# One head's rows of wo through six DMA engines, three heads of the last group as 1 KB rows

## The chip, the cores and the metric

The kernel runs on one core of a Trainium2 chip. The metric is the device time of one execution in microseconds (us). Executions of one kernel do not agree exactly, so a comparison here is of several executions of two kernels in alternation on one chip. A ratio is the mean time of one kernel's fast runs over that of the other's fast runs of the same rounds, so it is not quite the ratio of the medians quoted beside it.

## The reference

Decode attention with grouped heads over a window of 512 cached positions, then the output projection:

```python
B, Sq, D = 32, 1, 512;  Hq, Hkv, Sk, Dh = 32, 8, 2048, 128;  W = 512
q = (x @ wq).reshape(B, Sq, Hq, Dh)
scores = q . k[:, :, Sk-W:] * Dh**-0.5;  p = softmax(scores);  o = p @ v[:, :, Sk-W:]
out = o.reshape(B, Sq, Hq*Dh) @ wo          # wo: 4096 x 512, bf16, 4 MB
```

The bytes are 33.6 MB each of K and V, 4.2 MB each of wq and wo: 75.5 MB, nearly all read once.

## The kernel before: the parts that matter

The last thing loaded is wo, eight groups of 512 rows (one group = four heads). A partition takes four neighbouring rows, one piece of 4 KB. Because of that a partition m holds rows 4m to 4m+3, and the attention output must be brought into the same order: a *selection* by matmuls with a band of ones gives `o_sel[m, i, group, batch]`.

```python
            sp.wait_ge(pe_PV, 2 * Z_HOME.rindex("w") + 2)
            for hg in range(NHG):                       # NHG = 8 groups
                for i0, i1 in ((0, 4),) if hg < NHG - 1 else ((0, WO_CUT), (WO_CUT, 4)):
                    sp.dma_start(wo_sb[:, hg, i0:i1]..., wo[hg*512:(hg+1)*512, :].rearrange("(m i) n -> m (i n)", i=4)...)
                      .then_inc(sem_last if i0 else sem_wo[hg], 16)
# ... TensorE, after the last V chunk (V15) has been used:
            select(SELCUT, B, ...)                      # 4 x 4 matmuls, 128x128 weights
            pe.wait_ge(dve_sel, 2); pe.wait_ge(act_sel, 2)
            for hg in range(NHG):
                pe.wait_ge(sem_wo[hg], 16)
                for i in range(4):
                    if hg == NHG - 1 and i == WO_CUT:   # WO_CUT = 3
                        pe.wait_ge(sem_last, 16)
                    for c in range(2):                  # two halves of 256 columns
                        pe.matmul(X_ps[32*c:32*(c+1), 2, 0:256], lhsT=o_sel[:, i, hg, :], rhs=wo_sb[:, hg, i, c*256:(c+1)*256], ...)
```

A selection of the first 24 batches is done earlier, the last 8 batches only after V15.

Of the kernel before, what the change touches and what calls it, by code (L numbers as in the profile page):

```python
# [5 lines left out]
BF16 = mybir.dt.bfloat16  # L6
F32 = mybir.dt.float32
ACTF = mybir.ActivationFunctionType
ALU = mybir.AluOpType
# [3 lines left out]
def bass_standalone__sliding_block_cached__sampling_kernel(  # L13
# [8 lines left out]
    B, Sq, D = x.shape  # L22
    _, HKV, SK, DH = k_cache.shape
    HD = wq.shape[1]
    HQ = HD // DH
# [19 lines left out]
    RING = 3  # L45
    WO_CUT = 3
    XD = 20
# [24 lines left out]
    with ExitStack() as es:  # L72
# [12 lines left out]
        pick = sb("pick", [P, REP, KS + P], BF16)  # L85
        mask = sb("mask", [P, NBG], F32)
        oT_sb = sb("oT_sb", [P, HQ, B], BF16)
        ident = sb("ident", [32, 32], BF16)
# [7 lines left out]
        K_0 = K_sb[:, 0].rearrange("p r d -> p (r d)")  # L96
        o_sel = K_0[:, 0:HQ * B].rearrange("p (i g b) -> p i g b", i=4, g=NHG)
        band = K_0[:, HQ * B:HQ * B + 4 * 224].rearrange("p (i n) -> p i n", i=4)
        oT_flat = oT_sb[:, :, :].rearrange("p h b -> p (h b)")
# [22 lines left out]
        sem_wq = [sem(f"sem_wq{i}") for i in range(2)]  # L122
        sem_wo = [sem(f"sem_wo{i}") for i in range(NHG)]
        sem_last = sem("sem_last")
        sem_k = [sem(f"sem_k{i}") for i in range(NK)]
# [31 lines left out]
        pool_band = sem("pool_band")  # L157
        pool_qbd = sem("pool_qbd")
        nc.scalar.dma_start(x_sb, x.rearrange("b s d -> b (s d)")).then_inc(sem_x, 16)
        wq_rows = wq.rearrange("(p t) n -> p (t n)", t=DKT)  # L160
# [16 lines left out]
        def z_waits(eng, q):  # L177
# [7 lines left out]
            else:  # L185
                eng.wait_ge(pe_S, NQUAD)

        def cache_rows(cache, m, k=1):
            q, e = divmod(m, 2)
            rows = cache[4 * q:4 * q + 4, :, SK - W:, :].rearrange("b g (s r) d -> (b g) s (r d)", s=KS)  # L190
            return rows[:, :, e * CR * DH:(e + k) * CR * DH]

        @block.sync
        def _(sp):
# [19 lines left out]
            sp.wait_ge(pe_PV, 2 * Z_HOME.rindex("w") + 2)  # L214
            for hg in range(NHG):
                for i0, i1 in ((0, 4),) if hg < NHG - 1 else ((0, WO_CUT), (WO_CUT, 4)):
                    sp.dma_start(  # L217
                        wo_sb[:, hg, i0:i1].rearrange("p i n -> p (i n)"),
                        wo[hg * 512:(hg + 1) * 512, :].rearrange("(m i) n -> m (i n)", i=4)[:, i0 * 512:i1 * 512],
                    ).then_inc(sem_last if i0 else sem_wo[hg], 16)  # L220
            sp.wait_ge(dve_out, 1)
# [7 lines left out]
        def _(pool):  # L229
# [43 lines left out]
            for q in range(NQUAD):  # L273
# [3 lines left out]
            pool.memset(band[:, :, :], 0.0).then_inc(pool_band, 1)  # L277
            pool.wait_ge(pool_band, 1)
            pool.affine_select(
                out=band[:, :, :], in_=band[:, :, :], compare_op=ALU.not_equal, fill=1.0,  # L280
                base=384, pattern=[[-1, 4], [-4, 224]], channel_multiplier=1,
            ).then_inc(pool_band, 1)

        @block.tensor
        def _(pe):
# [82 lines left out]

            def select(b0, b1, dst):
                pe.wait_ge(act_O, min(b1 // 4, NQUAD - 1))  # L370
                if b1 == B:
                    pe.wait_ge(dve_O, 1)
                for i in range(4):
                    for hi in range(4):
                        ins = pe.matmul(
                            dst(i),
                            lhsT=band[:, i, 96 - 32 * hi:224 - 32 * hi],
                            rhs=oT_sb[:, :, b0:b1].rearrange("p (g hi) b -> p hi g b", hi=4)[:, hi],
                            start=(hi == 0), stop=(hi == 3), tile_position=(0, 0), skip_group_check=True,
                        )  # L380
                ins.then_inc(pe_sel, 1)

            for name in PE_ORDER:
                k = int(name[1:])
                {"S": scores, "P": p_turn, "V": pv}[name[0]](k)
                if name == "V12":
                    pe.wait_ge(pool_band, 2)
                    nb = SELCUT
                    select(0, nb, lambda i: X_ps[:, i // 2, (i % 2) * NHG * nb:(i % 2 + 1) * NHG * nb])
            nl = B - SELCUT  # L390
            select(SELCUT, B, lambda i: S_ps[:, i // 2, (i % 2) * NHG * nl:(i % 2 + 1) * NHG * nl])
            pe.wait_ge(dve_sel, 2)
            pe.wait_ge(act_sel, 2)
            for hg in range(NHG):
                pe.wait_ge(sem_wo[hg], 16)
                for i in range(4):
                    if hg == NHG - 1 and i == WO_CUT:
                        pe.wait_ge(sem_last, 16)
                    for c in range(2):
                        ins = pe.matmul(  # L400
                            X_ps[32 * c:32 * (c + 1), 2, 0:256],
                            lhsT=o_sel[:, i, hg, :],
                            rhs=wo_sb[:, hg, i, c * 256:(c + 1) * 256],
                            start=(hg == 0 and i == 0), stop=(hg == NHG - 1 and i == 3),
                            tile_position=(0, 32 * c),
                        )
            ins.then_inc(pe_fin, 1)

        @block.vector
        def _(dve):  # L410
# [62 lines left out]
            def sel_evac(src, i0, ni, b0, b1):  # L473
                return (
                    o_sel[:, i0:i0 + ni, :, b0:b1],
                    src[:, 0:ni * NHG * (b1 - b0)].rearrange("p (i g b) -> p i g b", i=ni, g=NHG),
                )

            dve.wait_ge(pe_sel, 1)
            dve.tensor_copy(*sel_evac(X_ps[:, 0], 0, 2, 0, SELCUT)).then_inc(dve_sel, 1)  # L480
            dve.wait_ge(pe_PV, NCH)
            dve.tensor_copy(  # L482
# [3 lines left out]
            dve.wait_ge(pe_sel, 2)  # L486
            dve.tensor_copy(*sel_evac(S_ps[:, 0], 0, 2, SELCUT, B)).then_inc(dve_sel, 1)
            dve.wait_ge(pe_fin, 1)
            dve.tensor_copy(out_sb[:, 0, :], X_ps[0:32, 2, 0:256]).then_inc(dve_out, 1)

        @block.scalar
        def _(act):
# [52 lines left out]
            for name in ACT_ORDER:  # L545
                arg = [int(a) for a in name[1:].split(".")]
                {"E": soften, "N": norm, "C": pt_evac, "O": o_evac, "Z": spread}[name[0]](*arg)
                if name == "Z7.3":
                    act.wait_ge(pe_sel, 1)
                    act.activation(  # L550
                        o_sel[:, 2:4, :, 0:SELCUT],
                        X_ps[:, 1, 0:2 * NHG * SELCUT].rearrange("p (i g b) -> p i g b", i=2, g=NHG),
                        ACTF.Copy,
                    ).then_inc(act_sel, 1)
            nl = B - SELCUT
            act.wait_ge(pe_sel, 2)
            act.activation(
                o_sel[:, 2:4, :, SELCUT:B],
                S_ps[:, 1, 0:2 * NHG * nl].rearrange("p (i g b) -> p i g b", i=2, g=NHG),
                ACTF.Copy,  # L560
            ).then_inc(act_sel, 1)
            act.wait_ge(pe_fin, 1)
            act.activation(out_sb[:, 1, :], X_ps[32:64, 2, 0:256], ACTF.Copy).then_inc(act_out, 1)
# [28 lines left out]
```

## Time and profile before

| | before |
|---|---|
| median time | 187.2 us (187.12 to 187.27) |
| span of the profiled run | 185.5 us |
| HBM read | 75.53 MB, 407 GB/s over the span |
| last V load landed, its first matmul | 172.57 us, 172.70 us |
| last wo load landed, TensorE's end | 182.72 us, 183.06 us |

Times within a run count from the start of the span. The prediction below shows the lines that carry the reading. Two things that no view prints are taken from the trace directly: how long single DMA packets took (a packet is one record of the trace's DMA part, with its size and duration), and the completions. In the trace every large load has 16 completions, each with its time. I call them *landings* and read each as one DMA engine's: the page counts 16 DMA engines, and the distances between landings hold from load to load (the last of the 16 lies 3.39 to 3.44 us behind the first in each of the first seven groups of wo). I count a load as there at its last landing: V15's last landing before is 172.57 us, its first matmul starts at 172.70.

### The profile page before, as it was taken

What the parts mean: (1) busy time and instruction counts of PE and PEld (TensorE: products, weight loads), DVE (VectorE), ACT (ScalarE), POOL (GpSimd) and SP (SyncE); (2) the same over time, 40 slices, a digit from 0 to 9 for tenths busy, and PEclk for the clock granted to TensorE, in tenths of its full rate; (3) what the DMA queues carried; (4) which work ended last, traced back from release to release, by engine and by line L of the source; (5) the groups of instructions that cost most, each with busy time, mean ns of one, the idle gap of its engine ahead of it and who ended that gap; (6) DMA issues with size and microseconds to landing.
All of it is one profiled execution on the core that took longest, in us unless ns stands there. A gap on an engine that the chain in (4) does not pass through costs nothing.

```text
span 185.5 us, 3711 instructions
## 1 busy us (share of the span) xinstructions
PE 109.5 (59%) x1540; PEld 90.3 (49%) x1540; DVE 132.1 (71%) x239; ACT 81.2 (44%) x141; POOL 31.8 (17%) x82
## 2 busy tenths in 40 slices
PE   0220303454469704994430899155999989998773
PEld 0100001141369403974130878014998888997761
DVE  0018699979799799979999269999999975510020
ACT  3000100129900686027941005965939999961000
POOL 7100029515300250042330015000003000000000
PEclk9999999999559965799965599755599999999999
DMA  6999999989999999999999999989999999999980
GB/s 201 428 445 424 431 421 484 445 367 424 424 421 445 413 435 421 428 435 410 458 438 392 445 410 442 463 382 442 415 431 431 410 438 417 438 410 416 400 338 30
DMA packets 5872, 75.80 MB, mean 409 GB/s; under 512 B 672, under 2 KB 864, under 8 KB 1888
## 3 DMA queue, kind: packets, MB, share of 16 engines
q1 hardware_dynamic: 5808, 75.53, 96.5%
q8 instruction: 12, 0.20, 0.4%
q10 hardware_dynamic: 48, 0.03, 0.1%
q14 instruction: 4, 0.03, 0.0%
HBM read 75.53 MB, written 0.03 MB: 407 GB/s over the span
## 4 chain that ended last, share of the span: by engine, by line
DMA 41%; PE 22%; DVE 20%; ACT 7%; issue 6%; SPq 3%
PE O_ps L361 16%; DMA V_sb<-in_v_cache_dram 11%; DMA w_sb<-in_wo_dram 11%; DVE KT_sb L439 10%; DMA K_sb<-in_k_cache_dram 10%; DMA w_sb<-in_wq_dram 9%; DVE w_sb L461 5%; PE S_ps L322 4%; ACT w_sb L530 4%; DVE QA_sb L429 2%; SPq L217 2%; ACT KT_sb L530 1%; PE PT_ps L341 1%; DVE maxv L446 1%; PE X_ps L302 1%
## 5 line engine op out<-in xcount | busy, mean ns | idle before, releaser
L439 DVE STREAM_TRANSPOSE KT_sb<-K_sb 128x2048 uint32<-128x2048 uint32 x32 | 72.5, 2290 | 12.9 <-DMA K_sb<-in_k_cache_dram 12.9
L361 PE MATMUL O_ps<-w_sb,V_sb 128*128 128x128 bf16 x640 | 45.4, 240 | 10.0 <-DVE w_sb L461 5.1
L361 PEld LDWEIGHTS O_ps<-w_sb,V_sb 128*128 128x128 bf16 x640 | 44.2, 108 | 12.0 <-issue 6.1
L271 POOL COPY QBD<-QA_sb 32x64 bf16<-32x64 bf16 x64 | 25.5, 539 | 83.0 <-PE S_ps L322 60.5
L530 ACT ACTIVATE w_sb<-PTc,mask 128x512 bf16<-128x512 bf16 x60 | 38.7, 725 | 0.0
L461 DVE TENSOR_SCALAR w_sb<-PTc,mask 128x512 bf16<-128x512 bf16 x100 | 31.1, 379 | 2.3 <-ACT PTc L521 1.1
L322 PE MATMUL S_ps<-KT_sb,QBD 128*32 128x512 bf16 x256 | 20.2, 465 | 18.2 <-POOL QBD L271 11.0
L341 PE MATMUL PT_ps<-P_bf,pick 128*128 128x128 bf16 x128 | 12.6, 277 | 24.6 <-ACT P_bf L511 20.0
L341 PEld LDWEIGHTS PT_ps<-P_bf,pick 128*128 128x128 bf16 x128 | 10.9, 128 | 28.2 <-ACT P_bf L511 22.8
L502 ACT ACTIVATE X_ps<-S_ps,negmax 128x512 f32<-128x512 f32 x8 | 5.2, 649 | 39.5 <-DVE negmax L448 39.5
L322 PEld LDWEIGHTS S_ps<-KT_sb,QBD 128*32 128x32 bf16 x256 | 7.5, 108 | 27.7 <-POOL QBD L271 11.9
L361 PE MATMUL O_ps<-K_sb,V_sb 128*128 128x128 bf16 x256 | 15.1, 217 | 2.3 <-DMA V_sb<-in_v_cache_dram 2.3
L530 ACT ACTIVATE K_sb<-PTc,mask 128x512 bf16<-128x512 bf16 x24 | 15.3, 717 | 1.6 <-DVE KT_sb L439 1.6
L361 PEld LDWEIGHTS O_ps<-K_sb,V_sb 128*128 128x128 bf16 x256 | 14.5, 96 | 3.1 <-issue 3.1
L540 ACT ACTIVATE oT_sb<-O_ps 128x128 bf16<-128x128 f32 x7 | 5.2, 742 | 16.9 <-PE O_ps L361 16.9
L461 DVE TENSOR_SCALAR K_sb<-PTc,mask 128x512 bf16<-128x512 bf16 x40 | 10.7, 346 | 2.4 <-ACT PTc L521 2.4
L302 PE MATMUL X_ps<-w_sb,oT_sb 128*32 128x512 bf16 x32 | 3.8, 627 | 10.6 <-DMA w_sb<-in_wq_dram 10.6
L482 DVE CAST oT_sb<-O_ps 128x128 bf16<-128x128 f32 x1 | 0.7, 711 | 12.9 <-PE O_ps L361 12.9
L496 ACT ACTIVATE KT_sb<-X_ps 128x512 bf16<-128x512 f32 x1 | 0.6, 597 | 17.3 <-PE X_ps L302 17.3
L511 ACT ACTIVATE P_bf<-X_ps,recip 128x512 bf16<-128x512 f32 x8 | 5.5, 682 | 6.0 <-DVE recip L454 6.0
L530 ACT ACTIVATE KT_sb<-PTc,mask 128x512 bf16<-128x512 bf16 x12 | 8.0, 726 | 0.0
L361 PE MATMUL O_ps<-KT_sb,V_sb 128*128 128x128 bf16 x128 | 7.5, 217 | 0.7 <-DMA V_sb<-in_v_cache_dram 0.7
(43 smaller groups left out, 56.0 us busy)
## 6 DMA issues: line engine op xcount, KB each, us to landing
K_sb<-in_k_cache_dram SPq DMA_DIRECT2D x16, 2048.0 KB, 15.0
V_sb<-in_v_cache_dram SPq DMA_DIRECT2D x10, 2048.0 KB, 15.4
V_sb<-in_v_cache_dram SPq DMA_DIRECT2D x3, 4096.0 KB, 23.4
w_sb<-in_wq_dram SPq DMA_DIRECT2D x2, 2048.0 KB, 11.8
w_sb<-in_wo_dram SPq DMA_DIRECT2D x7, 512.0 KB, 18.2
w_sb<-in_wo_dram SPq DMA_DIRECT2D x1, 384.0 KB, 21.0
w_sb<-in_wo_dram SPq DMA_DIRECT2D x1, 128.0 KB, 17.5
oT_sb<-in_x_dram ACTq DMA_DIRECT2D x1, 32.0 KB, 4.4
```

Of the source, the lines that this page charges most:

```text
L217: sp.dma_start(wo_sb[:, hg, i0:i1].rearrange("p i n -> p (i n)"), wo[hg * 512:(hg + 1) * 512, :].rearrange("(m i) n -> m (i n)", i=4)[:, i ...
L271: pool.tensor_copy(dst[:, i, :, x0:x0 + 4], src).then_inc(pool_qbd, 1)
L302: ins = pe.matmul(X_ps[32 * c:32 * c + 32, k, :], lhsT=xT_sb[:, kt, :], rhs=w_sb[:, kt, c * 1024 + k * 512:c * 1024 + (k + 1) * 512], star ...
L322: ins = pe.matmul(S_ps[32 * c:32 * c + 32, q % 2, :], lhsT=QBD[:, q % 2, g, b, e, :], rhs=bass.AP(tensor=KT_sb, offset=s0 * slot + (b * G ...
L341: ins = pe.matmul(PT_ps[:, r, :], lhsT=pick[:, r, KS - s:KS - s + P], rhs=P_bf[:, s, :], start=(s == 0), stop=(s == KS - 1), tile_position ...
L361: ins = pe.matmul(O_ps[:, q % 2, 0:P], lhsT=V_sb[:, m % NV, r, :], rhs=z_of(q)[:, :, x0 + r, :], start=(e == 0 and r == 0), stop=(e == 1 a ...
L439: dve.transpose(KT_w[:, n % NK, b].rearrange("p i r s -> p r i s"), K_w[:, n % NK, :, 32 * b:32 * b + 32],).then_inc(dve_T, 1)
L461: ins = dve.tensor_scalar(z_of(q)[:, k].rearrange("p x r -> p (x r)"), PTc[:, q % RING].rearrange("p x r -> p (x r)"), mask[:, k:k + 1], N ...
L502: act.activation(P_f32, S_ps[:, q % 2, :], ACTF.Exp, bias=negmax[:, q:q + 1], scale=SCALE, accum_out=sums[:, q:q + 1],).then_inc(act_exp, 1)
L511: act.activation(P_bf[:, :, :], P_f32.rearrange("p (x s) -> p s x", s=KS), ACTF.Copy, scale=recip[:, q:q + 1],).then_inc(act_P, 1)
L530: ins = act.activation(z_of(q)[:, k].rearrange("p x r -> p (x r)"), PTc[:, q % RING].rearrange("p x r -> p (x r)"), ACTF.Copy, scale=mask[ ...
L540: act.activation(oT_sb[:, :, 4 * q:4 * q + 4].rearrange("p h a -> p a h"), O_ps[:, q % 2, 0:P].rearrange("p (a h) -> p a h", a=4), ACTF.Co ...
```

## The change

Its intent: the 16 DMA engines do not finish together (the landings of the last wo load before lie between 179.38 and 182.72 us), so give the early ones more and the late ones less. The first head of the last group (128 rows of wo, 128 KB) is stored as 16 rows of 8 KB and loaded by three issues of 6, 6 and 4 rows. In the trace these have 16 landings together, in six series, so I read that six DMA engines carry them. I call them the first six. The other three heads of that group are loaded as 128 rows of 1 KB each, in head order, so that `oT_sb` can be used directly without selection. The split head needs its own small selection (eight matmuls with 32 columns of weights, of which 16 are used) and eight projection steps with 32 rows of contraction.

```diff
-    WO_CUT = 3
+    NG = NHG - 1
+    H0 = 4 * NG
+    FEW = ((0, 6), (1, 6), (2, 4))
@@ loads
+            sp.wait_ge(pool_few, 1)
+            for part, n in FEW:
+                sp.dma_start(few_w[part:part + 4 * n - 3:4]..., wo[row:row + 8 * n, :].rearrange("(m i) n -> m (i n)", i=8))
+                  .then_inc(sem_few, 16)
+            for hg in range(NG): ...                     # seven groups as before
+            sp.dma_start(wo_sb[:, NG, 1:3], wo[(H0 + 1) * DH:(H0 + 3) * DH, :].rearrange("(h d) n -> d h n", h=2))
+            sp.dma_start(wo_sb[:, NG, 3], wo[(H0 + 3) * DH:, :]).then_inc(sem_last, 16)
@@ GpSimd (from 139 us on): band for the small selection, and few_w set to zero
+            pool.memset(few_band, 0.0); 3 x pool.affine_select(...); pool.memset(few_w, 0.0)
@@ select(): seven groups instead of eight, then
+                for i in range(8):
+                    pe.matmul(few(i), lhsT=few_band[:, i], rhs=oT_sb[:, H0, b0:b1], ...)
@@ projection
+            for hg in range(NG):
+                ... four steps each, and before the seventh group:
+                    for i in range(8): project(few_o[:, i, :], few_w[:, i], False, False)
+            for i in range(1, 4):
+                pe.wait_ge(sem_last if i == 3 else sem_wo[NG], 16)
+                project(oT_sb[:, H0 + i, :], wo_sb[:, NG, i], False, i == 3)
```

(Cut: evacuations of the small selection on VectorE and ScalarE, semaphores, tile declarations.)

More of the change, by code (lines that the diff above doesn't have):

```diff
@@ L86, in bass_standalone__sliding_block_cached__sampling_kernel @@
         mask = sb("mask", [P, NBG], F32)
+        few_o = sb("few_o", [32, 8, B], BF16)
         oT_sb = sb("oT_sb", [P, HQ, B], BF16)
@@ L97, in bass_standalone__sliding_block_cached__sampling_kernel @@
         o_sel = K_0[:, 0:HQ * B].rearrange("p (i g b) -> p i g b", i=4, g=NHG)
+        few_w = K_0[0:32, 4096:8192].rearrange("p (i n) -> p i n", i=8)
+        few_band = K_0[:, HQ * B + 4 * 224:HQ * B + 4 * 224 + 256].rearrange("p (i j s) -> p i j s", i=8, s=4)
         band = K_0[:, HQ * B:HQ * B + 4 * 224].rearrange("p (i n) -> p i n", i=4)
@@ L123, in bass_standalone__sliding_block_cached__sampling_kernel @@
         sem_wo = [sem(f"sem_wo{i}") for i in range(NHG)]
+        sem_few = sem("sem_few")
         sem_last = sem("sem_last")
@@ L158, in bass_standalone__sliding_block_cached__sampling_kernel @@
         pool_qbd = sem("pool_qbd")
+        pool_few = sem("pool_few")
+        dve_few = sem("dve_few")
+        act_few = sem("act_few")
         nc.scalar.dma_start(x_sb, x.rearrange("b s d -> b (s d)")).then_inc(sem_x, 16)
@@ L186, in z_waits, with few_evac @@
                 eng.wait_ge(pe_S, NQUAD)
+        def few_evac(src, i0, b0, b1):
+            n0 = 2 * NG * (b1 - b0)
+            return (
+                few_o[:, i0:i0 + 4, b0:b1],
+                src[:, n0:n0 + 4 * (b1 - b0)].rearrange("p (i b) -> p i b", i=4),
+            )
         def cache_rows(cache, m, k=1):
@@ L214, in _ @@
             sp.wait_ge(pe_PV, 2 * Z_HOME.rindex("w") + 2)
-            for hg in range(NHG):
-                for i0, i1 in ((0, 4),) if hg < NHG - 1 else ((0, WO_CUT), (WO_CUT, 4)):
-                    sp.dma_start(
-                        wo_sb[:, hg, i0:i1].rearrange("p i n -> p (i n)"),
-                        wo[hg * 512:(hg + 1) * 512, :].rearrange("(m i) n -> m (i n)", i=4)[:, i0 * 512:i1 * 512],
-                    ).then_inc(sem_last if i0 else sem_wo[hg], 16)
+            sp.wait_ge(pool_few, 1)
+            first = 0
+            for part, n in FEW:
+                row = H0 * DH + 8 * first
+                sp.dma_start(
+                    few_w[part:part + 4 * n - 3:4].rearrange("p i n -> p (i n)"),
+                    wo[row:row + 8 * n, :].rearrange("(m i) n -> m (i n)", i=8),
+                ).then_inc(sem_few, 16)
+                first += n
+            for hg in range(NG):
+                sp.dma_start(
+                    wo_sb[:, hg].rearrange("p i n -> p (i n)"),
+                    wo[hg * 512:(hg + 1) * 512, :].rearrange("(m i) n -> m (i n)", i=4),
+                ).then_inc(sem_wo[hg], 16)
+            sp.dma_start(
+                wo_sb[:, NG, 1:3], wo[(H0 + 1) * DH:(H0 + 3) * DH, :].rearrange("(h d) n -> d h n", h=2)
+            ).then_inc(sem_wo[NG], 16)
+            sp.dma_start(wo_sb[:, NG, 3], wo[(H0 + 3) * DH:, :]).then_inc(sem_last, 16)
             sp.wait_ge(dve_out, 1)
@@ L277, in _ @@
             pool.memset(band[:, :, :], 0.0).then_inc(pool_band, 1)
-            pool.wait_ge(pool_band, 1)
+            pool.memset(few_band[:, :, :, :], 0.0).then_inc(pool_band, 1)
+            pool.wait_ge(pool_band, 2)
             pool.affine_select(
@@ L282, in _ @@
             ).then_inc(pool_band, 1)
+            for part, _ in FEW:
+                spots = few_band[:, :, 0:6, part]
+                pool.affine_select(
+                    out=spots, in_=spots, compare_op=ALU.not_equal, fill=1.0,
+                    base=-48 * part, pattern=[[-1, 8], [-8, 6]], channel_multiplier=1,
+                ).then_inc(pool_band, 1)
+            pool.memset(few_w.rearrange("p i n -> p (i n)"), 0.0).then_inc(pool_few, 1)
         @block.tensor
@@ L367, in pv, with few_at, select @@
                 ins.then_inc(pe_PV, 1)
-            def select(b0, b1, dst):
+            def few_at(ps, nb):
+                n0 = 2 * NG * nb
+                return lambda i: ps[0:32, i // 4, n0 + (i % 4) * nb:n0 + (i % 4 + 1) * nb]
+            def select(b0, b1, dst, few):
                 pe.wait_ge(act_O, min(b1 // 4, NQUAD - 1))
@@ L377, in select @@
                             lhsT=band[:, i, 96 - 32 * hi:224 - 32 * hi],
-                            rhs=oT_sb[:, :, b0:b1].rearrange("p (g hi) b -> p hi g b", hi=4)[:, hi],
+                            rhs=oT_sb[:, 0:H0, b0:b1].rearrange("p (g hi) b -> p hi g b", hi=4)[:, hi],
                             start=(hi == 0), stop=(hi == 3), tile_position=(0, 0), skip_group_check=True,
                         )
+                for i in range(8):
+                    ins = pe.matmul(
+                        few(i),
+                        lhsT=few_band[:, i].rearrange("p j s -> p (j s)"),
+                        rhs=oT_sb[:, H0, b0:b1],
+                        start=True, stop=True, tile_position=(0, 0), skip_group_check=True,
+                    )
                 ins.then_inc(pe_sel, 1)
@@ L386, in _ @@
                 if name == "V12":
-                    pe.wait_ge(pool_band, 2)
+                    pe.wait_ge(pool_band, 3 + len(FEW))
                     nb = SELCUT
-                    select(0, nb, lambda i: X_ps[:, i // 2, (i % 2) * NHG * nb:(i % 2 + 1) * NHG * nb])
+                    select(
+                        0, nb, lambda i: X_ps[:, i // 2, (i % 2) * NG * nb:(i % 2 + 1) * NG * nb], few_at(X_ps, nb)
+                    )
             nl = B - SELCUT
-            select(SELCUT, B, lambda i: S_ps[:, i // 2, (i % 2) * NHG * nl:(i % 2 + 1) * NHG * nl])
+            select(
+                SELCUT, B, lambda i: S_ps[:, i // 2, (i % 2) * NG * nl:(i % 2 + 1) * NG * nl], few_at(S_ps, nl)
+            )
@@ L392, in _, with project @@
             pe.wait_ge(dve_sel, 2)
             pe.wait_ge(act_sel, 2)
-            for hg in range(NHG):
+            def project(lhsT, rhs, start, stop):
+                for c in range(2):
+                    ins = pe.matmul(
+                        X_ps[32 * c:32 * (c + 1), 2, 0:256],
+                        lhsT=lhsT, rhs=rhs[:, c * 256:(c + 1) * 256],
+                        start=start, stop=stop, tile_position=(0, 32 * c),
+                    )
+                return ins
+            for hg in range(NG):
@@ L395, in _ @@
                 pe.wait_ge(sem_wo[hg], 16)
                 for i in range(4):
-                    if hg == NHG - 1 and i == WO_CUT:
-                        pe.wait_ge(sem_last, 16)
-                    for c in range(2):
-                        ins = pe.matmul(
-                            X_ps[32 * c:32 * (c + 1), 2, 0:256],
-                            lhsT=o_sel[:, i, hg, :],
-                            rhs=wo_sb[:, hg, i, c * 256:(c + 1) * 256],
-                            start=(hg == 0 and i == 0), stop=(hg == NHG - 1 and i == 3),
-                            tile_position=(0, 32 * c),
-                        )
+                    project(o_sel[:, i, hg, :], wo_sb[:, hg, i], hg + i == 0, False)
@@ L407, in _ @@
+                if hg == NG - 2:
+                    pe.wait_ge(dve_few, 2)
+                    pe.wait_ge(act_few, 2)
+                    pe.wait_ge(sem_few, 16 * len(FEW))
+                    for i in range(8):
+                        project(few_o[:, i, :], few_w[:, i], False, False)
+            for i in range(1, 4):
+                pe.wait_ge(sem_last if i == 3 else sem_wo[NG], 16)
+                ins = project(oT_sb[:, H0 + i, :], wo_sb[:, NG, i], False, i == 3)
             ins.then_inc(pe_fin, 1)
@@ L474, in sel_evac @@
                 return (
-                    o_sel[:, i0:i0 + ni, :, b0:b1],
-                    src[:, 0:ni * NHG * (b1 - b0)].rearrange("p (i g b) -> p i g b", i=ni, g=NHG),
+                    o_sel[:, i0:i0 + ni, 0:NG, b0:b1],
+                    src[:, 0:ni * NG * (b1 - b0)].rearrange("p (i g b) -> p i g b", i=ni, g=NG),
                 )
@@ L480, in _ @@
             dve.tensor_copy(*sel_evac(X_ps[:, 0], 0, 2, 0, SELCUT)).then_inc(dve_sel, 1)
+            dve.tensor_copy(*few_evac(X_ps[0:32, 0], 0, 0, SELCUT)).then_inc(dve_few, 1)
             dve.wait_ge(pe_PV, NCH)
@@ L487, in _ @@
             dve.tensor_copy(*sel_evac(S_ps[:, 0], 0, 2, SELCUT, B)).then_inc(dve_sel, 1)
+            dve.tensor_copy(*few_evac(S_ps[0:32, 0], 0, SELCUT, B)).then_inc(dve_few, 1)
             dve.wait_ge(pe_fin, 1)
@@ L550, in _ @@
                     act.activation(
-                        o_sel[:, 2:4, :, 0:SELCUT],
-                        X_ps[:, 1, 0:2 * NHG * SELCUT].rearrange("p (i g b) -> p i g b", i=2, g=NHG),
+                        o_sel[:, 2:4, 0:NG, 0:SELCUT],
+                        X_ps[:, 1, 0:2 * NG * SELCUT].rearrange("p (i g b) -> p i g b", i=2, g=NG),
                         ACTF.Copy,
                     ).then_inc(act_sel, 1)
+                    act.activation(*few_evac(X_ps[0:32, 1], 4, 0, SELCUT), ACTF.Copy).then_inc(act_few, 1)
             nl = B - SELCUT
@@ L557, in _ @@
             act.activation(
-                o_sel[:, 2:4, :, SELCUT:B],
-                S_ps[:, 1, 0:2 * NHG * nl].rearrange("p (i g b) -> p i g b", i=2, g=NHG),
+                o_sel[:, 2:4, 0:NG, SELCUT:B],
+                S_ps[:, 1, 0:2 * NG * nl].rearrange("p (i g b) -> p i g b", i=2, g=NG),
                 ACTF.Copy,
             ).then_inc(act_sel, 1)
+            act.activation(*few_evac(S_ps[0:32, 1], 4, SELCUT, B), ACTF.Copy).then_inc(act_few, 1)
             act.wait_ge(pe_fin, 1)
```

## The prediction

The sums: for TensorE they came to 182.07 + 0.33 + 0.75 + 0.30 = 183.45 us, for DMA to 182.48 + 0.05 + 0.05 + 0.27 = 182.85 us. That the split head's rows go to six engines was my assumption at that point; the 0.15 us for a change of tiling mode is my estimate from the 0.09 and 0.27 us of the trace.

> **What bounds the kernel now.** I read the page's slices first. They show the DMA engines busy from the second slice to the third from last, so the whole span is one long transfer and only its tail can be shortened.
>
> ```profile
> DMA  6999999989999999999999999989999999999980
> GB/s 201 428 445 424 431 421 484 445 367 424 424 421 445 413 435 421 428 435 410 458 438 392 445 410 442 463 382 442 415 431 431 410 438 417 438 410 416 400 338 30
> ```
>
> The bytes do not change (75.5 MB), so the question is how the last microseconds are spent. Second, the chain in order of time, at its end: after the last V load is issued the chain runs through the issues of wo, then waits 21.03 us for wo itself, then does eight matmuls and an eviction.
>
> ```profile
> 161.37 21.03 DMA w_sb<-in_wo_dram
> 182.40 0.04 issue
> 182.45 0.63 PE X_ps L400 x8
> 183.08 0.02 issue
> 183.10 0.41 DVE oT_sb L489
> ```
>
> Third, the timeline from 172 us, which shows the other half of the tail, the computing that must follow the last V load:
>
> ```profile
> 172.70 3.77 PE L361 MATMUL O_ps<-K_sb,V_sb 128*128 128x128 bf16 x64 [1.17 <-DMA V_sb<-in_v_cache_dram]
> 176.51 0.71 DVE L482 CAST oT_sb<-O_ps 128x128 bf16<-128x128 f32 x1 [12.88 <-PE O_ps L361]
> 177.37 0.63 PE L375 MATMUL S_ps<-oT_sb,K_sb 128*128 128x64 bf16 x16 [0.90 <-DVE oT_sb L482]
> 178.03 0.29 DVE L487 CAST K_sb<-S_ps 128x128 bf16<-128x128 f32 x1 [0.81 <-PE S_ps L375]
> 178.41 2.80 PE L400 MATMUL X_ps<-w_sb,K_sb 128*32 128x256 bf16 x48 [0.41 <-DVE K_sb L487]
> 181.51 0.61 PE L400 MATMUL X_ps<-w_sb,K_sb 128*32 128x256 bf16 x8 [0.30 <-DMA w_sb<-in_wo_dram]
> 182.45 0.61 PE L400 MATMUL X_ps<-w_sb,K_sb 128*32 128x256 bf16 x8 [0.33 <-DMA w_sb<-in_wo_dram]
> ```
>
> The reader is to see that six of the eight groups of the output projection run without a gap, and that only the last two wait for DMA, 0.30 and 0.33 us each. Hence two paths end almost together. Without DMA waits PE would need 63 steps of 0.0538 us (2.80 us less the last one's 0.272, over 47) plus 0.272: 178.41 + 3.39 + 0.27 = 182.07. It ended at 183.06. The **slack of PE is 1.0 us**; a gain on the DMA side is capped by it, and PE work added behind the last V load eats it.
>
> Fourth, the stretches of 1 us at the end:
>
> ```profile
> 178.00:179.00 1.00, 0.59 (x12) 0.62 (x14) 0.29 (x1) 0.28 (x1) 0.00 (x0) 1.00 1.01 394
> 179.00:180.00 1.00, 1.00 (x24) 1.00 (x20) 0.00 (x0) 0.00 (x0) 0.00 (x0) 1.00 0.69 270
> 180.00:181.00 1.00, 1.00 (x23) 0.92 (x18) 0.00 (x0) 0.00 (x0) 0.00 (x0) 1.00 0.49 178
> 181.00:182.00 1.00, 0.70 (x12) 0.32 (x8) 0.00 (x0) 0.00 (x0) 0.00 (x0) 1.00 0.19 75
> 182.00:183.00 1.00, 0.68 (x12) 0.31 (x8) 0.00 (x0) 0.00 (x0) 0.00 (x0) 1.00 0.05 17
> ```
>
> The column before the last is the DMA share. It falls from 1 to 0 over 3.5 us: the 16 engines do not finish together. The trace keeps the 16 landings of every issue. For the last issue they lie at 179.38 to 179.68 (five engines), 180.10 (two), 180.90 to 181.38 (six) and 182.66 to 182.72 (three); for the load at 32 us all 16 lay within 0.35 us. The steps come from the page's instruction queue:
>
> ```profile
> q8 instruction: 12, 0.20, 0.4%
> ```
>
> These are 12 packets of 16 KB. After each of them one engine's landings are some 1.5 us later than before, for good, and after each of four 8 KB packets 0.75 us. By 178 us three engines have had two 16 KB packets. They are the last.
>
> [...] 4 KB packets take 0.159 to 0.172 us, 3 KB ones 0.121 and more, 1 KB ones 0.046. [...] from L361 to L322 (128x128 to 128x32) successive matmuls start 0.147 us apart instead of 0.056, and from L322 back to L361 0.32 to 0.33 us.
>
> **The change part by part.** *DMA of the ten uninvolved engines.* Before, the last group cost each engine 8 x 0.122 + 8 x 0.046 + two completions of 0.009 = 1.36 us. After it is 24 packets of 1 KB: 24 x 0.046 + 0.018 = 1.12 us. They end **0.24 us earlier**: the three late ones at 182.72 - 0.24 = 182.48. *The first six engines* take three, or two, rows of 8 KB more, about 0.32 us each (twice a 4 KB packet): +0.96 - 0.24 = 0.7 us later. If they are among the early ones (179.4 to 180.1) they end by 180.8 and nothing waits for them. The trace gives no engine numbers; I choose to believe it, since the design makes sense only then.
>
> *PE, second selection.* The 16 matmuls shrink from 64 to 56 columns, but took 0.0295 us each at a size where little is saved; I count nothing. Eight new ones with 32 columns of weights at 0.03 each are 0.24 us, and the mode change before them 0.09 us. The semaphore that the evictions wait for is given after the eighth, so all of it, **0.33 us**, lies on the path. The small extra evictions follow the main ones and are needed only 48 matmuls later: hidden.
>
> *PE, projection.* 64 matmuls become 56 + 16 + 6 = 78: 14 x 0.0538 = **0.75 us** more. The 16 have 32 rows of contraction, another tiling mode between two stretches of 128x32: two changes, which I size at 0.15 us each (between the 0.09 and 0.27 of the trace[...]): **0.30 us**.
>
> *Sum for PE.* Free-running end 182.07 + 0.33 + 0.75 + 0.30 = **183.45**, against 183.06 before. *Sum for DMA.* 182.48, then one wait, two matmuls: 182.48 + 0.05 + 0.05 + 0.27 = **182.85**. The later one counts: 183.45, that is +0.39 us, or some +0.25 if my sizes of mode changes and small matmuls are a little high. The PE would then meet every wo group already landed.
>
> *Off the path.* GpSimd gets a memset of 256 columns, three selects and a memset of 32x4096, by its rate here (0.843 us for 896 columns) about 4 us; it starts at 139 us and the loads that need it are not issued before 157.9. The first selection gets eight matmuls too (some 0.3 us net), but the PE waits 1.13 us for V data before L361 at 167.77, which swallows it. Three more issues at 0.43 us each on the queue: issued at 158, needed from 169.
>
> **The rivals.** *(A) DMA stays the bound:* the mode changes are free and the small selections overlap; then the end is 182.85 to 183.0 and the time 187.0. For it: the projection waits for DMA now. Against it: the 1.0 us slack is smaller than the 14 + 8 extra matmuls plus switches. *(B) The first six engines include a late one:* that one ends 0.7 us after 182.72, then 0.34 us of work: 183.8, time 187.9 to 188.0. *(C) The twelfth instruction block moves:* it was fetched at 180.82, when PE was about 45 matmuls into the projection, and met an engine almost done. With 16 more matmuls ahead of it, it comes at about 180.2, meets an engine that has 0.9 us of work left, and delays that one by 1.5 us to some 182.5. That equals the three late ones: no gain lost, but no slack either. *(D) The GpSimd work slows VectorE at 139 to 146 us:* hidden behind the 1.1 us waits for V.
>
> **Range and chances.** Weights: PE-bound near +0.3 about 65%, DMA-bound near -0.2 about 20%, B about 10%, rest noise (before spread 0.15 us). I give **187.45 us**, range **187.0 to 187.9**. Two per cent is 3.7 us, more than the whole tail after the last V load can move, so within 2% has 0.98, faster 0.01, slower 0.01.
>
> **What would show each step.** In the trace after: the last landing of the last wo issue near 182.5 (DMA step); the last issue's landings of the first six engines below 181.5 (choice of engines); the selection at the end lasting 0.9 to 1.0 us instead of 0.63; the projection's matmuls in one run without "DMA w_sb<-in_wo_dram" waits, ending near 183.4; gaps of 0.1 to 0.2 us on either side of the 32-row matmuls. The chain that ends last should go through PE and the last V load instead of wo. The prediction is wrong if the chain still ends in the wo DMA, if the landing of the last V load (172.57 us before) moves by more than a few tenths, or if instruction fetches fall on other engines or other moments.

## The result

The changed kernel took 187.44 us median (187.24 to 187.76, 4 runs) against 187.24 us (4 runs), ratio 1.0013 with a 95% interval of 0.9996 to 1.0031. Timed again in five more rounds (after_again below): 187.44 against 187.26 us, ratio 1.0007 (0.9995 to 1.0020). It is neither faster nor clearly slower.

The slices of the changed kernel look as before: the DMA engines are full up to the last slices.

```profile
DMA  6999999989999999999999999999999999999980
GB/s 215 413 452 417 431 441 462 452 371 413 448 406 438 424 420 441 417 431 427 432 445 402 434 427 431 455 417 409 425 427 424 427 424 427 431 420 403 405 320 26
```

The chain that ended last has changed its course (start, duration, what). Before, its last long piece was the wait for wo; now it is the wait for V, and from there on the chain is TensorE's own work:

```profile
158.14 14.34 DMA V_sb<-in_v_cache_dram
...
172.62 3.78 PE O_ps L397 x64
...
177.28 0.57 PE S_ps L415 x16
177.85 0.30 PE S_ps L422 x8
...
178.54 4.76 PE X_ps L448 x78
...
183.32 0.41 DVE oT_sb L552
```

The timeline of the same stretch shows how nearly the two limits meet:

```profile
181.28 1.05 PE L448 MATMUL X_ps<-K_sb,few_o 32*32 32x256 bf16 x16
182.26 0.61 PE L448 MATMUL X_ps<-w_sb,K_sb 128*32 128x256 bf16 x8
182.71 0.57 PE L448 MATMUL X_ps<-w_sb,oT_sb 128*32 128x256 bf16 x6
182.99 0.10 PEld L448 LDWEIGHTS X_ps<-w_sb,oT_sb 128*32 128x32 bf16 x2 [0.18 <-DMA w_sb<-in_wo_dram]
```

TensorE runs 76 matmuls without a DMA wait, but the weights of the very last two are held until 182.99 us by a wo load whose last landing is 182.95 us. That is 0.23 us *later* than the last landing before (182.72 us), although the late engines were to be relieved. In the profile of the repetition the last landing was 182.88 us, and no wait was left: TensorE started its projection at 178.63 and ended it at 183.27 us.

The cause stands in the landings. At the end there are three late engines at 182.14, 182.22 and 182.36 us, and a fourth at 182.95. The three issues of the split head have 16 landings, which fall into six series with steps of 0.30 to 0.35 us, one for each engine. Five of the six series begin at 169.58, 169.58, 170.07, 170.32 and 171.63 us; the sixth, with two rows, has 171.21 and 171.53 us. (Four series have three rows and two have two; numbered as in the probe below, those of two are engines 4 and 5. The other one is early, 169.58 and 169.91 us.) A group of wo takes an engine 1.28 us, so this engine should land the first group at 172.8 us. No landing of that group is there; the odd one out is at 174.33 us, 1.5 us later, and the eleventh of the 12 packets of 16 KB in the queue "q8 instruction" starts at 171.32 us. (I call these packets TensorE's instruction blocks: between the first and the last of the 12, TensorE starts 2814 matmuls and weight loads, some 256 to a packet, in both kernels.) So I read that the block fell on this engine, which had already had one (its share of V15, the last V load, landed at 170.90 us, 1.6 us behind the earliest), and carries 16 KB of the split head besides. The probe and the five-engine variant below say that it is engine 5: the probe finds engine 4 early, and without rows on engine 5 the last landing falls.

### The profile page after: what moved, and what is told of

It reads as the page before. It is cut to its first block, busy times and chain, and to the rows that moved or that the text cites. A ratio compares the mean times of both kernels' runs of the same rounds, so it can differ in the third digit from the quotient of the medians.

```text
span 185.7 us, 3788 instructions
## 1 busy us (share of the span) xinstructions
PE 112.9 (61%) x1570; PEld 92.3 (50%) x1570; DVE 136.6 (74%) x241; ACT 81.7 (44%) x143; POOL 37.4 (20%) x87
## 4 chain that ended last, share of the span: by engine, by line
DMA 38%; PE 27%; DVE 26%; issue 6%; ACT 2%; SPq 1%; DVEq 0%
DMA V_sb<-in_v_cache_dram 19%; PE O_ps L397 17%; DVE KT_sb L500 10%; DVE w_sb L522 10%; DMA K_sb<-in_k_cache_dram 10%; DMA w_sb<-in_wq_dram 9%; PE S_ps L358 4%; PE X_ps L448 3%; DVE QA_sb L490 2%; DVE maxv L507 1%; PE PT_ps L377 1%; PE X_ps L338 1%; ACT P_bf L574 1%; ACT KT_sb L593 1%; SPq L220 1%
## 5 line engine op out<-in xcount | busy, mean ns | idle before, releaser
L397 PE MATMUL O_ps<-w_sb,V_sb 128*128 128x128 bf16 x640 | 46.3, 242 | 8.9 <-DVE w_sb L522 6.0
L397 PEld LDWEIGHTS O_ps<-w_sb,V_sb 128*128 128x128 bf16 x640 | 45.0, 110 | 11.0 <-DVE w_sb L522 7.0
L299 POOL COPY QBD<-QA_sb 32x64 bf16<-32x64 bf16 x64 | 26.1, 549 | 82.1 <-PE S_ps L358 59.7
L522 DVE TENSOR_SCALAR w_sb<-PTc,mask 128x512 bf16<-128x512 bf16 x100 | 35.5, 426 | 1.9 <-ACT PTc L584 1.1
L358 PE MATMUL S_ps<-KT_sb,QBD 128*32 128x512 bf16 x256 | 21.5, 489 | 18.1 <-POOL QBD L299 11.0
L507 DVE TENSOR_REDUCE maxv<-S_ps 128x1 f32<-128x512 f32 x8 | 5.5, 686 | 3.5 <-PE S_ps L358 3.4
```

The source lines that it names most:

```text
L299: pool.tensor_copy(dst[:, i, :, x0:x0 + 4], src).then_inc(pool_qbd, 1)
L358: ins = pe.matmul(S_ps[32 * c:32 * c + 32, q % 2, :], lhsT=QBD[:, q % 2, g, b, e, :], rhs=bass.AP(tensor=KT_sb, offset=s0 * slot + (b * G ...
L397: ins = pe.matmul(O_ps[:, q % 2, 0:P], lhsT=V_sb[:, m % NV, r, :], rhs=z_of(q)[:, :, x0 + r, :], start=(e == 0 and r == 0), stop=(e == 1 a ...
L507: dve.tensor_reduce(maxv[:, q:q + 1], S_ps[:, q % 2, :], AX.X, ALU.max).then_inc(dve_sm, 1)
L522: ins = dve.tensor_scalar(z_of(q)[:, k].rearrange("p x r -> p (x r)"), PTc[:, q % RING].rearrange("p x r -> p (x r)"), mask[:, k:k + 1], N ...
```

## The experiments

Theories after the first look. **P:** the added TensorE work sets the end, the DMA side has slack. **D:** the last landing sets the end, because one of the first six engines is itself late. **Tie:** both ends lie within 0.1 us, so that moving one alone does nothing. All ratios are to the kernel before in the same rounds.

| run | what it is | median us | before us | ratio (95%) | V15 starts | last wo landing |
|---|---|---|---|---|---|---|
| after_again | the changed kernel, repeated | 187.44 | 187.26 | 1.0007 (0.9995 to 1.0020) | 172.71 | 182.88 |
| e1_even | split head on all 16 engines | 188.14 | 187.13 | 1.0071 (1.0042 to 1.0100) | 173.65 | 183.66 |
| e2_nofewpe | without the small matmuls | 187.42 | 187.13 | 1.0007 (0.9995 to 1.0019) | 172.79 | 182.90 |
| e3_probe | before + 15 tiny loads | 188.46 (one run) | 187.13 | none | 172.59 | 183.88 |
| e4_pe36 | before + 36 matmuls | 188.11 | 187.13 | 1.0051 (1.0038 to 1.0064) | 172.69 | 182.68 |
| e5_five | split head on five engines | 187.39 | 187.28 | 1.0007 (0.9994 to 1.0020) | 172.72 | 182.44 |
| e6_five_nope | both | 187.04 | 187.28 | 0.9985 (0.9973 to 0.9998) | 172.87 | 182.55 |
| e7_k8 | split head on eight engines | 187.45 | 187.26 | 1.0009 (0.9993 to 1.0024) | 172.59 | 182.92 |
| e8_contig | same engines, other partitions | 187.97 | 187.28 | 1.0039 (1.0025 to 1.0053) | 173.03 | 183.55 |
| b1_five_last | before, a quarter group meant for five engines | 187.23 | 187.28 | 1.0001 (0.9987 to 1.0014) | 172.53 | 182.79 |
| b2_rows4 | 32 rows of 4 KB on five engines | 186.92 | 187.26 | 0.9983 (0.9970 to 0.9996) | 172.60 | 182.39 |

(Engine counts are the rows of an issue, as the probe's landings count them; the two last columns are from the profiled run of each; runs of one chip: e1 to e4; e5, e6, e8, b1; after_again, e7, b2.)

### How much TensorE work fits behind the last V load

```diff
+            pe.wait_ge(sem_wo[0], 16)
+            for j in range(36):
+                pe.matmul(O_ps[32*(j%2):..., 1, 256:512], lhsT=o_sel[:, 0, 0, :], rhs=wo_sb[:, 0, 0, ...], ...)   # unused output
             for hg in range(NHG):
```

> The kernel before with 36 matmuls of the projection's shape added ahead of the projection, into unused PSUM: 36 x 0.0538 = 1.94 us of TensorE work. If TensorE had 1.0 us of slack behind the last V load, as read from the profile, the time rises by 0.9 to 1.0 us to 188.2 us. If there was no slack: by 1.9 us to 189.1 us. If DMA alone sets the end: no change, 187.2 us.

It rose by 0.98 us (188.11 against 187.13). The timeline of this run shows the added block and then all 64 matmuls in one go, with no wait for wo left between them:

```profile
178.39 2.14 PE L397 MATMUL O_ps<-w_sb,K_sb 128*32 128x256 bf16 x36 [0.41 <-DVE K_sb L496]
180.35 3.67 PE L409 MATMUL X_ps<-w_sb,K_sb 128*32 128x256 bf16 x64
```

So of 1.94 us added, 0.96 us vanished in waits: the slack of 1.0 us that the prediction read from the profile is shown.

### Which engines are late

```diff
+            for n in range(1, 16):
+                sp.dma_start(tiny[0:n, n - 1], wo[0:n, 0:64]).then_inc(sem_tiny[n - 1], 16)
             for hg in range(NHG):
```

> The kernel before with 15 tiny loads ahead of wo, the n-th of n rows of 128 bytes, each with its own semaphore[...]. If my choice in the prediction holds, the three engines that end last are numbered 6 or above and all six first ones are among the early ones. Rival (theory D): at least one of engines 0 to 5 has fetched TensorE instruction blocks and lies 1.5 us or more behind the earliest. Time 187.2 to 187.5 us, as issuing 15 loads at 0.43 us each is hidden.

The trace has n landings for the n-th tiny load, and those of one engine follow each other at 0.18 us. So I read that each load adds one engine, and I number the engines in this order: engine n is the one that the load of n+1 rows adds. That a load of few rows in another kernel goes to the same engines is my assumption; the run without rows on engine 5 below agrees with it (last landing 182.44 instead of 182.95 us). Engine 0 lands its first tiny load at 169.28 us, the fourth load adds engine 3 at 171.36, the fifth adds engine 4 at 169.61, the sixth adds engine 5 at **172.63**, the seventh engine 6 at 172.65, the eighth engine 7 at 169.43 us. Taking off 0.18 us for the tiny load itself, engine 5's V15 share landed at 172.45 us and engine 6's at 172.47; the two latest landings of V15 in this run are at 172.43 and 172.46 us, so these are the two late ones. Engines 1 and 2 lie 0.9 and 1.0 us behind engine 0, engine 3 lies 2.1 us behind, engines 4, 7 and 8 are early. Engine 5's share landed 3.35 us behind engine 0's (169.10 after the same subtraction), and a block sets an engine back by some 1.5 us (in the kernel before, the landings of a load spread over 0.36 us ahead of the first block, at 44.3 us, and over 1.79 us in the load behind it). So I read that **engine 5 is one of those that the instruction blocks fall on**, and the choice of the first six engines contains it. The time was a miss of my expectation: 188.46 us, 1.3 us above the kernel before, in one run. The tiny rows of one engine landed 0.18 us apart (engine 0: 169.28, 169.46, 169.64, 169.83), though a packet of 128 bytes took only 0.013 us. What they cost the load behind them is between the two: engine 5, with ten rows, landed its first group of wo 2.54 us after its V15 share (172.45 and 174.99 us), where a group takes 1.28, so 1.26 us for ten.

### Taking away the TensorE work, the late engine, and both

Without the small matmuls (result wrong; one head is missing):

```diff
-                for i in range(8):
-                    ins = pe.matmul(few(i), lhsT=few_band[:, i]..., rhs=oT_sb[:, H0, b0:b1], ...)
@@
-                    for i in range(8):
-                        project(few_o[:, i, :], few_w[:, i], False, False)
```

> The changed kernel without the 2 x 8 small selection matmuls and the 16 projection matmuls of the split head (wrong result on purpose: one head is missing); all DMA as in the changed kernel. Theory P: the TensorE path shortens by 0.24 + 0.9 us and the time falls well below both kernels, to 186.5 to 186.8 us. Theory D: the last landing near 182.9 us still holds the last two matmuls, end at 183.25, time unchanged at 187.3 to 187.4 us, with about 1 us of waits for wo in the projection.

Some 1.4 us of TensorE work are gone (0.30 for the small selection, 16 x 0.0538 and two mode changes of 0.1 for the projection) and the time is unchanged (1.0007, as the repeated changed kernel). The timeline shows where the room went: into waits for wo.

```profile
182.04 0.61 PE L441 MATMUL X_ps<-w_sb,K_sb 128*32 128x256 bf16 x8 [0.70 <-DMA w_sb<-in_wo_dram]
182.63 0.60 PE L441 MATMUL X_ps<-w_sb,oT_sb 128*32 128x256 bf16 x6
182.94 0.10 PEld L441 LDWEIGHTS X_ps<-w_sb,oT_sb 128*32 128x32 bf16 x2 [0.20 <-DMA w_sb<-in_wo_dram]
```

So P alone is refuted. Next, engine 5 without rows of the split head:

```diff
-    FEW = ((0, 6), (1, 6), (2, 4))
+    FEW = ((0, 5), (1, 5), (2, 4), (3, 2))
```

> The changed kernel with its 16 rows of 8 KB dealt to the first five engines (5, 5, 4 and 2 rows) instead of the first six, so that engine 5, which the probe showed among the late ones, carries none. TensorE work as in the changed kernel. Theory tie (TensorE and the last landing end together): the last landing falls from 182.9 to about 182.4 us, but the TensorE run still ends at 183.2 to 183.3 us and the time stays at 187.3 to 187.4 us. Theory D alone (the last landing sets the end): the time falls by 0.5 us to 186.9 us.

The last landing fell to 182.44 us, as foreseen, and the time did not (1.0007). TensorE now runs through to the end and waits for nothing:

```profile
178.64 2.80 PE L449 MATMUL X_ps<-w_sb,K_sb 128*32 128x256 bf16 x48 [0.40 <-DVE K_sb L550]
181.36 1.05 PE L449 MATMUL X_ps<-K_sb,few_o 32*32 32x256 bf16 x16
182.34 0.61 PE L449 MATMUL X_ps<-w_sb,K_sb 128*32 128x256 bf16 x8
182.79 0.49 PE L449 MATMUL X_ps<-w_sb,oT_sb 128*32 128x256 bf16 x6
```

D alone is refuted too. Both edits together:

> As the five-engine variant, and without the small selection and projection matmuls of the split head (wrong on purpose). Theory tie: with both limits moved the time falls at last, by about 0.5 us, to 186.8 to 186.9 us, with the last matmuls held by landings near 182.4 us. Theory P alone would have shown this drop already without moving the rows, and theory D alone would show no difference to the five-engine variant with its matmuls.

Measured 187.04 us, ratio 0.9985. It is the only one of the four combinations (1.0007 to 1.0013, 1.0007, 1.0007, 0.9985) below the kernel before. Against the five-engine variant, of the same rounds, that is 0.0022 of the time, 0.41 us (my expectation of 186.8 to 186.9 us was a little low). The **tie** holds: in the changed kernel TensorE's work and the last landing end together, and each hides a gain on the other.

### Where the rows are written

```diff
-    FEW = ((0, 6), (1, 6), (2, 4))
+    FEW = ((0, 16),)
-                    few_w[part:part + 4 * n - 3:4]
+                    few_w[part:part + 2 * n - 1:2]        # row r into partition 2r; band changed to match
```

> The changed kernel with its 16 rows of 8 KB spread over all 16 DMA engines (one row each) instead of the first six; TensorE does exactly the work of the changed kernel. Theory P (the added TensorE work sets the end): no change against the changed kernel, 187.4 us, projection again one run of about 4.7 us from 178.5 us. Theory D (the last wo landing sets the end, 182.95 us in the changed kernel, because one of the first six engines is itself late): the late engines now land at about 182.5 to 182.7 us, all within 0.3 us, and the time falls with the last landing by 0.25 us to 187.2 us. Tie (both ends within 0.1 us): lower by at most 0.05 us.

All three theories missed: 188.14 us, 1.0 us (0.5%) above the kernel before by the medians; the ratio of means says 0.7% because one of the six runs took 189.91 us. The chain shows V15's 64 matmuls a whole microsecond later than in the changed kernel (172.62), and everything behind shifted with them:

```profile
173.65 3.78 PE O_ps L397 x64
...
179.57 4.66 PE X_ps L448 x78
```

Its V load had its last landing at 173.51 us instead of 172.48. In the changed kernel an engine's rows land after its share of V15 (the six series begin some 0.3 us after V15 landings at 169.27, 169.27, 169.76, 170.01, 170.90 and 171.32 us), so its own row does not hold up its own share. But the early rows are written while V15 is still under way: they land from 169.58 us on, V15's last landing is at 172.48. And the partitions differ: in the changed kernel row j of an issue goes into partition 4j, 4j+1 or 4j+2, in the even variant row r into partition 2r. That the destination partitions delay V15 was a guess of mine, which I call theory W. The test keeps engines, bytes and the place in the queue and alters only the partitions:

```diff
-                    few_w[part:part + 4 * n - 3:4]        # row j -> partition 4j + part
+                    few_w[first:first + n]                # row j -> partition first + j
```

> The changed kernel with the same rows on the same six engines at the same time, but put into partitions 0 to 15 in order instead of partitions 0, 4, 8 and so on[...]. Theory W (in the even variant the last V load landed 1 us late[...]): the last V load lands later than 172.5 us, by 0.3 us or more, and the time rises to 187.7 to 188.4 us. Rival (the even variant was late only because the late engines got 8 KB rows too, 0.3 us each): nothing changes, 187.4 us.

187.97 us, 0.53 us above the changed kernel's 187.44 (0.69 us above the kernel before in its own rounds), and V15 started at 173.03 us. A counter-test uses more engines, among them two late ones, but again every fourth partition (`FEW = ((0, 8), (1, 8))`, row j into partition 4j or 4j+1):

> The changed kernel with its 16 rows on the first eight engines, two each[...]. Theory W: the last V load lands at 172.5 us as in the changed kernel[...]. Rival (any row on a late engine delays the V load): 172.8 us or later. Engine choice: engines 5 and 6, late in the probe, both carry 16 KB more, so the last landing comes at 182.9 to 183.3 us and the time is 187.4 to 187.8 us, not below the changed kernel.

V15 started at 172.59 us, the last landing was 182.92, the time 187.45 us. The first timeline line is of the variant with partitions 0 to 15, the second of the one with eight engines and every fourth partition:

```profile
173.03 3.77 PE L398 MATMUL O_ps<-K_sb,V_sb 128*128 128x128 bf16 x64 [1.63 <-DMA V_sb<-in_v_cache_dram]
```

```profile
172.59 3.77 PE L398 MATMUL O_ps<-K_sb,V_sb 128*128 128x128 bf16 x64 [1.19 <-DMA V_sb<-in_v_cache_dram]
```

The start of V15 alone would be weak evidence, since it lies between 172.53 and 172.87 us in the profiles of all the runs but these two late ones. Nor does it hang on when V15 was issued: 158.68 us with partitions 0 to 15, but 158.80 us in the run without small matmuls on five engines, which started V15 at 172.87. The packets settle it. From 169 to 173 us the DMA engines were as busy with partitions 0 to 15 (first line) as in the changed kernel (second line), but moved less; the last two columns are DMA share and GB/s:

```profile
169.00:173.00 4.00, 2.40 (x43) 2.22 (x40) 0.00 (x0) 0.00 (x0) 0.00 (x0) 1.00 0.97 330
```

```profile
169.00:173.00 4.00, 2.85 (x51) 2.71 (x49) 0.00 (x0) 0.00 (x0) 0.00 (x0) 1.00 0.99 397
```

Rows and V were both slowed. From 168.5 to 172.7 us the median 8 KB row took 0.309 us in the changed kernel and 0.375 us with partitions 0 to 15, the median 16 KB packet of V 0.613 and 0.732 us. In the even variant they took 0.357 and 0.749 us, in the eight-engine one 0.309 and 0.614 us.

So it is shown that the destination partitions, and not the engines or the bytes, slow the packets and delay the V load. Why they do, no run shows. It also gives a reason for the selection that the change pays for: rows that an early engine takes over delay nothing here when they go into every fourth partition (V15 started at 172.59 to 172.87 us with such rows, at 172.53 to 172.70 without them in the kernel before, e4 and b1), and then the contraction index lies in unusual places.

### Two attempts to do better

The first leaves TensorE's work as before and moves a quarter of the last group (1 KB rows of 125 partitions) to five engines; that five carry them was my assumption and is not shown here, and the 0.084 us of a 2 KB packet in the expectation is my estimate, midway between 0.046 and 0.122:

```diff
+  (3, 4, 0, 125, sem_five), (3, 4, 125, P, sem_five), (0, 2, 0, P, sem_wo[hg]), (2, 3, 0, P, sem_last)     # i0, i1, p0, p1
```

> The kernel before with no change of TensorE's work: of the last group of wo, one quarter (1 KB rows of 125 partitions) goes through the first five engines alone, so that the other eleven carry 7 KB per engine of the last group less 1 KB packets: 8 x 0.084 + 8 x 0.046 + 0.018 = 1.06 us instead of 1.36. If the DMA tail of the late engines sets the end of the kernel before (theory D), the last landing falls from 182.7 to 182.4 us and the time by 0.3 us to 186.9 us. If theory W holds for these rows as well[...]: 187.0 to 187.5 us.

187.23 us, ratio 1.0001: nothing gained. The last landing was 182.79 us. The groups ahead of it landed late, the sixth at 180.65 instead of 180.19 us before and the seventh at 181.86 instead of 181.46. Their packets were slower (from 177.5 to 181 us those of 4 KB took 0.185 us on average, before 0.163), as V's were in the even variant; whether the moved rows' partitions are the cause here too, no run isolates. The second attempt takes what the experiments taught: only the first five engines, every fourth partition within an issue as in the changed kernel, and rows of 4 KB in 32 of 64 partitions, which halves the small matmuls:

```diff
+    FEW = ((0, 5), (1, 5), (2, 5), (3, 5), (4, 5), (5, 5), (6, 2))
+                p0 = 32 * (part // 4) + part % 4          # row j -> partitions 4j..4j+3 and 32+4j..
-                for i in range(8):                        # selection and projection
+                for i in range(4):
```

> Built from both findings: the split head as 32 rows of 4 KB on the first five engines only[...], so that the selection takes 4 instead of 8 small matmuls and the projection 8 instead of 16. Theory tie: the TensorE run ends 4 x 0.04 + 8 x 0.054 = 0.6 us earlier than in the five-engine variant (182.7 instead of 183.3), the last landing stays near 182.4 to 182.5 us, and the time is 186.7 to 187.0 us, below both kernels by some 0.3 us. Theory D or P alone would have it equal to the five-engine variant, 187.4 us, or gain only a part.

186.92 us, ratio 0.9983 (0.9970 to 0.9996), result correct: 0.34 us below the kernel before in its rounds and 0.52 us below the changed kernel. The gain is small, and its interval only just excludes no change. The timeline shows the shorter middle piece, with the last two weights again held by wo:

```profile
181.18 0.61 PE L450 MATMUL X_ps<-K_sb,few_o 64*32 64x256 bf16 x8
181.72 0.61 PE L450 MATMUL X_ps<-w_sb,K_sb 128*32 128x256 bf16 x8
182.17 0.55 PE L450 MATMUL X_ps<-w_sb,oT_sb 128*32 128x256 bf16 x6
...
182.43 0.10 PEld L450 LDWEIGHTS X_ps<-w_sb,oT_sb 128*32 128x32 bf16 x2 [0.16 <-DMA w_sb<-in_wo_dram]
```

The repetition of the changed kernel ran beside these:

> The changed kernel itself, unchanged, timed in five more rounds beside the variants of this call, since the differences are of 0.1 per cent. Expected from its first four runs: 187.3 to 187.5 us, ratio to the kernel before 1.0005 to 1.002. One engine of the first six should again be among those that end last.

It took 187.44 us, ratio 1.0007. Engine 5's pattern came again: two rows at 171.18 and 171.50 us, the first group of wo only at 174.26 us, the last landing at 182.88 us.

## Why the prediction was right, and which step was not

The time was right: 187.45 us predicted, 187.44 measured. That the two meet to 0.01 us is luck: the sum gave 0.39 us more than before, which I shaded to 0.25, and the measured 0.20 has two ends within 0.1 us behind it where I had one. Point by point:

- **What bounds the kernel: right.** Two paths with 1.0 us of slack on TensorE; 36 added matmuls (1.94 us) cost 0.98 us.
- **Relief of the uninvolved engines: right.** Predicted 0.24 us. Counted from their last V landing, the two late engines ended 10.15 us later before (172.51 to 182.66, 172.57 to 182.72) and 9.88 us later after (172.34 to 182.22, 172.48 to 182.36): 0.27 us.
- **Choice of engines: wrong. This is the step that failed.** The prediction chose to believe that the first six engines are among the early ones and gave rival B, a late one among them, 10%. Engine 5 is a late one. Of B's size only a part came: the last landing rose by 0.23 us to 182.95, not by 0.7. B was worked out for three rows, but engine 5 carries two: 0.63 us (from 170.90 to 171.53) less the relief of 0.27 makes 0.36. Where the other 0.13 us went, the runs do not settle. So the DMA limit was 182.95 + 0.05 + 0.05 + 0.27 = 183.32 us where I had 182.85.
- **TensorE, selection: right in kind, 0.09 us too large.** Predicted 0.33 us more; the two pieces (0.57 + 0.30) replace 0.63: 0.24 us.
- **TensorE, projection: right.** Predicted 1.05 us more than 3.66, that is 4.71; it took 4.64 us in the repetition, where nothing held it, and 4.76 with the wait for the last landing. The changes of tiling mode cost about 0.1 us each, against 0.15 assumed: in the repetition the first 32-row matmul starts 0.203 us after the matmul before it, and the first one behind them 0.198 us after the last, where each pair of matmuls otherwise starts 0.106 us after the one before. The 0.27 us that the assumption leaned on was read too large: those 512-column matmuls come in groups of four, and the next group follows the last matmul of a group by some 0.20 us anyway, so that 0.32 to 0.33 us are only 0.12 more.
- **The sum: right, for a weaker reason than I gave.** Predicted TensorE end 183.45, measured 183.27 to 183.30. The predicted margin over the DMA side, 0.6 us, was in truth within 0.1: "PE would then meet every wo group already landed" holds in the repetition and fails by one wait in the first profile.
- **Rival C (the twelfth instruction block):** it came at 180.15 us as worked out (180.2), but no engine fell back by 1.5 us through it; between the last two issues the largest change of one engine's distance is about 0.1 us. Presumably the engine that it fell on had next to nothing left to load; which one that was, the trace does not say.
- **Rival D (GpSimd slows VectorE): VectorE was slower in that stretch, and it was hidden.** The same 20 multiplications, before and after:

```profile
139.34 6.24 DVE L461 TENSOR_SCALAR w_sb<-PTc,mask 128x512 bf16<-128x512 bf16 x20 [0.56 <-PE O_ps L361]
```

```profile
138.92 10.00 DVE L522 TENSOR_SCALAR w_sb<-PTc,mask 128x512 bf16<-128x512 bf16 x20 [0.43 <-PE O_ps L397]
```

GpSimd is busy for 6.48 us of the 10 us from 139 to 149 us instead of 1.82. That its work is the cause of the 3.8 us more for 20 instructions, no run isolates. The last V load was issued at 158.14 instead of 157.31 us, but the DMA engines had work throughout (share 0.99 from 158 to 172 us) and V15 started at 172.62 instead of 172.70: nothing came of it. GpSimd's new work was also sized too small, again without effect: about 4 us predicted, 5.1 measured (0.46, 1.00 and 3.65 us).

What stays open: engine 5's two blocks did not come at the same moments in the probe (both before V15 had landed) and in the changed kernel (the second at 171.3 us). What decides which engine a block falls on, no run here tells, and so a choice of engines that is good for one program may not be for another.

## What to carry to other kernels

When two paths end together, test them in pairs: removing 1.4 us of TensorE work alone gave nothing, relieving the late DMA engine alone gave nothing, both gave 0.4 us. Before work is moved to "the early engines", measure which they are, engine by engine, with loads of one row, two rows and so on, whose landings the trace counts. And look at where a small load writes as well as at who carries it: the same rows in other partitions cost 0.5 us, and the delay showed in another load.
